# Sparse attention into an MoE layer: 17 pieces of weight conversion in two steps of the first chunk, and w_in's tiles one further ahead of w_out's

## The chip, the cores and the metric

The kernel runs on one core of a Trainium2 chip, with its engines TensorE (PE), VectorE (DVE), ScalarE (ACT), GpSimd (POOL) and SyncE (SP). The metric is the device time of one execution, in microseconds, taken as the median of several runs. Each engine works through its own instructions in order; semaphores tie the engines to each other and to the DMAs.

## What is computed

An attention layer with a block mask feeds a feed-forward layer. 4 batches, 8 heads, 768 positions, head size 64; blocks of 32 positions, each of which sees its neighbours, the first and last block, and three sampled blocks. The inputs are float32 and the weights `w_in` (512 x 2048) and `w_out` (2048 x 512) are too, as the reference stores them:

```python
scores = scale * np.matmul(q, k.transpose(0, 1, 3, 2))
scores = np.where(mask, scores, -1000000000.0)
attn = exp(scores - max) / (sum + 1e-09)
x = np.matmul(attn, v)            # heads joined: 3072 x 512
h = x @ w_in                      # 3072 x 2048
g = h * (1.0 / (1.0 + np.exp(-1.702 * h)))
out = (g @ w_out).astype(np.float32)
```

(The lines of the reference are shortened here.)

## The kernel before

The weights come as 64-bit words, two 32-bit halves each, 128 rows at a time: 16 tiles of w_in and 16 of w_out, 512 KB each (NF = 16). The kernel turns each into float32 and then into a high and a low part for matmuls in fp32r. Every product of the MoE layer is three matmuls: high by high, high by low, low by high.

**Chunks, items, steps.** The 3072 tokens are worked in NC = 6 chunks of 512. The attention of a chunk is a list of items, one for each unit of 64 query rows (the dense edge units have several). The first chunk's items are done ahead (`first`, L658). Then 6 x 16 = 96 MoE steps run, one `tick(m)` each (L618): step m multiplies the chunk by w_in tile m mod 16 (`up`, L482: 12 matmuls, L491 to L493, into PSUM bank 7), applies the gate (`gate`, L496: Tanh on ScalarE at L499, in the first 13 steps a copy of the bank at L504, a product on VectorE at L506), splits the result into ghi (L511, ScalarE) and glo (L519, VectorE), and multiplies the tile of the step before by w_out (`down`, L522: L541, L542, then L537). The attention items of the next chunk are woven between these (`plan`, L579). In the first chunk a new item's scores (L260) come about every second step: steps 1, 3, 5, 7, 9, 11, 12 and 14. Such a step is called heavy here, the others light. An item is four minima on VectorE (L283), four exponentials on ScalarE (L290), eight transposes on TensorE (L306) in the next step, two copies of them (pt, L310), the products with the values (L331), a normalisation (L373), and a turn of the result (L384) whose halves are stored by L391 and L392. The scores go into the two banks that the transposes of the item before went through, so they wait for the copies L310.

**The conversion of the weights.** `weights` (L401 on) is a generator that hands out one small piece of work for each call. Its list `todo` holds the 32 tiles in the order of their conversion: (f, 0) is w_in tile f and (f, 1) is w_out tile f. For the k-th tile it issues, in four calls:

1. the fetch of tile k + 2 (a DMA on ScalarE's queue, L414, into one of three buffers `raw`) and a shift on VectorE (L446, `shift`);
2. the last operation of tile k - 1 (a subtraction on VectorE, L427, `last`), which makes its low part, and, for a w_out tile, the save of its float32 form to DRAM (a DMA on ScalarE's queue, L433, out of the buffer `a`), from where later chunks load it again;
3. a bitwise combination on VectorE (L452, `or`), and on ScalarE the first operation of tile k + 1 (L422), which writes that tile's buffer `a`, one of three in turn;
4. a second combination on VectorE (L456, `or`) and the high part on ScalarE (L459).

The 16 w_in tiles stay in SBUF for good. The w_out tiles go round a ring of WRING = 3. So before it starts w_out tile f the generator asks whether the `down` of tile f - 3 has been issued (L441), and as long as it has not, a call does nothing (L442):

```python
while i == 1 and f - WRING > self.downs - 1:
    yield
```

**How many calls a step makes.** Before the loop, `first` makes 29 calls. In `tick`, n0 calls come ahead of `up`, n1 calls between the gate's ScalarE operations and its VectorE product L506, and n2 calls at the end of the step. A heavy step has no n0. If a tile were not ready in time, `need` (L464) would call the generator until it is. At step 16 what is left is issued at once (L699).

Since the order in which the instructions are issued is the order on each engine, a piece that is issued ahead of another one holds it up on its engine, whether it is urgent or not: the n1 calls stand ahead of the gate's product on VectorE and ahead of ghi on ScalarE, the n2 calls ahead of the next step's work.

Of the kernel before, what the change touches and what calls it, by code (L numbers as in the profile page):

```python
# [27 lines left out]
NF = DF // P  # L28
# [7 lines left out]
WRING = 3  # L36
LAG = 1
# [6 lines left out]
class Kernel:  # L44
# [353 lines left out]
    def weights(self):  # L398

        nc = self.nc  # L400
        todo = []  # L401
        for f in range(NF + LAG):
            if f < NF:
                todo.append((f, 0))
            if f >= LAG:
                todo.append((f - LAG, 1))
        self.ready = set()
        tiles = {}

        def fetch(k):  # L410
            if k < len(todo):
                f, i = todo[k]
                raw = self.work.tile([P, 2 * DM], I32, name="raw", bufs=3)
                nc.scalar.dma_start(out=raw, in_=self.w64[i][f])  # L414
                tiles[k] = {"raw": raw.rearrange("p (a b) -> p a b", b=2)}

        def first(k):


            if k < len(todo):  # L420
                a = tiles[k]["a"] = self.work.tile([P, DM], I32, name="a", bufs=3)
                nc.scalar.activation(out=a.bitcast(F32), in_=tiles[k]["raw"][:, :, 1].bitcast(F32), func=AF.Abs, scale=REBASE)  # L422

        def last(k):
            f, i = todo[k]
            t, w = tiles[k]["t"], tiles[k]["a"].bitcast(F32)
            nc.vector.tensor_tensor(out=t[:, DM:2 * DM], in0=w, in1=t[:, 0:DM].bitcast(F32), op=ALU.subtract)  # L427
            self.ready.add((f, i))

        def save(k):  # L430
            f, i = todo[k]
            if i == 1:
                nc.scalar.dma_start(out=self.ws[f], in_=tiles[k]["a"].bitcast(F32))  # L433
            del tiles[k]

        fetch(0)
        fetch(1)
        yield
        first(0)
        for k, (f, i) in enumerate(todo):  # L440
            while i == 1 and f - WRING > self.downs - 1:  # L441
                yield  # L442
            fetch(k + 2)
            raw, a = tiles[k]["raw"], tiles[k]["a"]
            low, high = raw[:, :, 0], raw[:, :, 1]
            nc.vector.tensor_scalar(out=a, in0=a, scalar1=3, scalar2=None, op0=ALU.logical_shift_left)  # L446
            yield
            if k > 0:
                last(k - 1)
                save(k - 1)  # L450
                yield
            nc.vector.scalar_tensor_tensor(out=a, in0=high, scalar=-0x80000000, in1=a, op0=ALU.bitwise_and,  # L452
                                           op1=ALU.bitwise_or)
            first(k + 1)
            yield
            nc.vector.scalar_tensor_tensor(out=a, in0=low, scalar=29, in1=a, op0=ALU.logical_shift_right,  # L456
                                           op1=ALU.bitwise_or)
            t = tiles[k]["t"] = self.win[f] if i == 0 else self.wout[f % WRING]
            nc.scalar.copy(out=t[:, 0:DM], in_=a.bitcast(F32))  # L459
            yield  # L460
        last(len(todo) - 1)
        save(len(todo) - 1)
# [155 lines left out]
    def tick(self, m):  # L618

        n0, n1, n2 = 0, 0, 0  # L620
        if m < NF:
            heavy = any(part == self.scores for q in range(QT) for part, g in self.at.get(QT * m + q, ()))
            n0, n1, n2 = (0, 3, 3) if heavy else (3, 3, 3)

        def run(n):
            for _ in range(n):
                next(self.conv, None)

        def finish(todo):
            for f in todo:  # L630
                f()

        moe = m < NC * NF
        self.gate_lo(m - 1)
        after = self.begin(QT * m)
        finish(after[:3])
        run(n0)
        finish(after[3:])
        if moe:
            self.up(m, range(0, 2))  # L640
        finish(self.begin(QT * m + 1))
        if moe:
            self.up(m, range(2, 4))
        after = self.begin(QT * m + 2)
        if moe:
            self.gate(m, lambda: run(n1))
        finish(after[:2])
        self.down(m - LAG, 0)
        if moe:
            self.gate_hi(m)  # L650
        finish(after[2:])
        finish(self.begin(QT * m + 3))
        self.down(m - LAG, 1)
        self.split(m + 1)
        self.stream(m + 3)
        run(n2)

    def first(self):  # L658
# [12 lines left out]
        for n, g in enumerate(items):  # L671
            if n == 1:
                next(self.conv)
            exps = self.scores(g)
            exps.pop(0)()
            if n > 1:
                weights(2)
                finish(self.turn(items[n - 2]))
            if n > 0:
                finish(self.transposes(items[n - 1]))  # L680
            finish(exps)
            if n > 0:
                finish(self.values(items[n - 1]))
            self.loads()
            if n > 1:
                weights(2)
# [66 lines left out]
```

## Time and profile before

| | |
|---|---|
| median of 3 runs | 785.84 us (785.08 to 786.23) |
| the profiled execution | 782.75 us |
| its span, first to last instruction | 781.1 us |
| mean granted TensorE clock | 0.984 |

The profile is one execution, with the busy time of each engine, the chain of work that ended last, and each instruction's start. A row of the order of instructions reads: start in us, duration in us, engine, line of the kernel, operation, output <- inputs, shapes, how many were merged, and in brackets the idle time of the engine just before it and what ended it. Durations are from start to the confirmed end, so on one engine the next instruction can start before the end that a row shows. ACTq and SPq are the DMA issues of ScalarE's and SyncE's queues.

### The profile page before, as it was taken

The numbers are of one execution on the slowest core, as the hardware profiler recorded it, in microseconds if no ns is written. First come the engines' busy times: TensorE is split into PE (matmuls) and PEld (weight loads), VectorE is DVE, ScalarE is ACT, GpSimd is POOL, SyncE is SP. The second block draws the span as 40 slices with busy tenths as digits, with TensorE's granted clock in tenths as the row PEclk, the third lists the DMA queues.
The fourth block names the chain that finished last, engine by engine and source line by source line (L and its number), as shares of the span: only waits on it lengthen the run. The fifth ranks groups of instructions, "written<-read, shape, count | busy, mean of one in ns | idle before, by whom it ended". The sixth has DMA issues, their size and how long they took to land.

```text
span 781.1 us, 19264 instructions
## 1 busy us (share of the span) xinstructions
PE 738.6 (95%) x7584; PEld 571.7 (73%) x7584; DVE 412.8 (53%) x1076; ACT 383.5 (49%) x950; POOL 57.1 (7%) x85
## 2 busy tenths in 40 slices
PE   2667999999999999999999999999999999999996
PEld 1445787767777777787877877877777777888884
DVE  3387779887644354445445544444554444443332
ACT  1567667666545444444444544444545454333332
POOL 5122001101000001000000000000000000000000
PEclk9699999999999999999999999999999999999998
DMA  8998887786644437664534465435574321041112
GB/s 267 281 367 296 251 254 256 251 259 222 206 162 153 117 114 219 173 177 129 161 117 145 142 175 156 137 115 163 161 229 153 93 98 42 28 108 40 55 41 55
DMA packets 61117, 128.22 MB, mean 164 GB/s; under 512 B 7569, under 2 KB 26514, under 8 KB 60514
## 3 DMA queue, kind: packets, MB, share of 16 engines
q1 hardware_dynamic: 46882, 80.50, 33.9%
q0 software_dynamic: 7232, 25.51, 10.1%
q10 hardware_dynamic: 6912, 20.97, 8.1%
q8 instruction: 60, 0.98, 0.5%
q14 instruction: 31, 0.25, 0.1%
HBM read 116.47 MB, written 10.49 MB: 163 GB/s over the span
## 4 chain that ended last, share of the span: by engine, by line
PE 78%; DMA 7%; DVE 7%; ACT 4%; issue 2%; SPq 1%; ACTq 0%; DVEq 0%
PE bank L491 11%; PE bank L541 10%; PE bank L542 10%; PE bank L537 10%; PE bank L493 10%; PE bank L492 10%; PE bank L260 5%; PE bank L306 4%; PE bank L331 4%; DMA ws<-a 3%; DMA kg<-in_kb_dram 2%; PE bank L339 2%; PE bank L272 2%; DMA raw<-in_moe_w_in_dram 2%; DVE a L452 1%
## 5 line engine op out<-in xcount | busy, mean ns | idle before, releaser
L491 PE MATMUL bank<-xhi,win 128*128 128x512 f32 x384 | 158.4, 412 | 1.2 <-ACT xhi L391 0.9
L290 ACT ACTIVATE ex<-bank,nm 128x256 f32<-128x256 f32 (+1 forms) x208 | 99.7, 492 | 115.4 <-DVE nm L283 113.6
L506 DVE SCALAR_TENSOR_TENSOR g<-g,bank 128x512 f32<-128x512 f32 x83 | 57.1, 687 | 183.8 <-ACT g L499 183.8
L541 PE MATMUL bank<-wout,ghi 128*128 128x512 f32 x384 | 154.1, 401 | 0.0
L542 PE MATMUL bank<-wout,ghi 128*128 128x512 f32 x384 | 151.7, 395 | 0.0
L493 PE MATMUL bank<-xhi,win 128*128 128x512 f32 x384 | 151.0, 393 | 0.0
L492 PE MATMUL bank<-xlo,win 128*128 128x512 f32 x384 | 150.0, 391 | 0.0
L499 ACT ACTIVATE g<-bank 128x512 f32<-128x512 f32 x96 | 57.5, 599 | 146.4 <-PE bank L493 146.1
L537 PE MATMUL bank<-wout,glo 128*128 128x512 f32 x384 | 107.7, 394 | 0.0
L480 DVE TENSOR_TENSOR wout<-wst,wout 128x512 fp32r<-128x512 f32 x80 | 55.4, 693 | 79.7 <-ACT wout L479 78.7
L511 ACT CAST ghi<-g 128x512 fp32r<-128x512 f32 x96 | 59.7, 622 | 54.6 <-DVE g L506 54.6
L491 PEld LDWEIGHTS bank<-xhi,win 128*128 128x128 f32 x384 | 72.1, 188 | 18.7 <-ACT xhi L391 1.1
L537 PEld LDWEIGHTS bank<-wout,glo 128*128 128x128 f32 x384 | 72.4, 189 | 17.3
L493 PEld LDWEIGHTS bank<-xhi,win 128*128 128x128 f32 x384 | 72.1, 188 | 16.3
L283 DVE CUSTOM_DVE_ANT_1 bank<-bank,bias 128x256 f32<-128x256 f32 x176 | 73.8, 440 | 19.3 <-PE bank L260 16.2
L542 PEld LDWEIGHTS bank<-wout,ghi 128*128 128x128 f32 x384 | 72.5, 189 | 15.6
L541 PEld LDWEIGHTS bank<-wout,ghi 128*128 128x128 f32 x384 | 72.2, 188 | 16.0
L492 PEld LDWEIGHTS bank<-xlo,win 128*128 128x128 f32 x384 | 72.3, 188 | 13.3 <-DVE xlo L392 0.3
L216 POOL DMA_INDIRECT vown<-in_v_dram,vidx x44 | 43.7, 994 | 496.9 <-PE bank L331 385.5
L260 PE MATMUL bank<-kg,qt 64*32 64x256 f32 x1408 | 55.8, 416 | 17.6 <-DMA vmid<-in_v_dram 10.5
L310 ACT COPY pt<-bank 128x512 f32<-128x512 f32 (+1 forms) x120 | 61.1, 563 | 19.4 <-PE bank L306 19.3
L331 PEld LDWEIGHTS bank<-vown,pt 128*32 128x32 f32 x1408 | 43.8, 113 | 31.8 <-ACT pt L310 16.0
(75 smaller groups left out, 821.8 us busy)
## 6 DMA issues: line engine op xcount, KB each, us to landing
wst<-ws SPq DMA_DIRECT2D x80, 256.0 KB, 2.7
kg<-in_kb_dram SPq DMA_DIRECT2D x136, 128.0 KB, 3.2
kg<-in_kb_dram SPq DMA_DIRECT2D x22, 384.0 KB, 4.9
raw<-in_moe_w_in_dram ACTq DMA_DIRECT2D x16, 512.0 KB, 9.7
raw<-in_moe_w_out_dram ACTq DMA_DIRECT2D x16, 512.0 KB, 4.5
kg<-in_kT_dram SPq DMA_DIRECT2D x4, 1536.0 KB
vown<-in_vd_dram SPq DMA_DIRECT2D x8, 768.0 KB, 6.0
qt<-in_q_dram SPq DMA_DIRECT2D x22, 256.0 KB, 4.9
```

What stands on the lines that cost most here:

```text
L260: nc.tensor.matmul(sps[h][BLK * c:BLK * (c + 1), n * i:n * (i + 1)].rearrange("p (n s) -> p n s", s=BLK), self.qt[r][rows, bi, UT * pair + ...
L283: nc.vector.tensor_tensor_reduce(out=at, in0=at, in1=bias, scale=-SCALE, scalar=3.0e38, op0=ALU.add, op1=ALU.min, accum_out=un["nm"][:, ha ...
L290: nc.scalar.activation(out=ex, in_=sps[h][:, n * k:n * (k + 1)], func=AF.Exp, bias=un["nm"][:, half, c:c + 1], scale=-1.0, accum_out=un["r ...
L310: copies.append(lambda pt=pt, ps=ps, m=m: nc.scalar.copy(out=pt[:, 0:m], in_=ps[:, 0:m]))
L331: nc.tensor.matmul(av[BLK * c:BLK * (c + 1), 0, 2 * i + h], g["pt"][h][:, 2 * i + k, BLK * c:BLK * (c + 1)], src[:, at:at + D], start=(k = ...
L491: nc.tensor.matmul(h, wih[:, k], hi[:, k], start=(k == 0), stop=False)
L492: nc.tensor.matmul(h, wih[:, k], lo[:, k], start=False, stop=False)
L493: nc.tensor.matmul(h, wil[:, k], hi[:, k], start=False, stop=(k == NCT - 1))
L511: self.nc.scalar.copy(out=ghi, in_=self.g[m][0])
L537: nc.tensor.matmul(o[n], glo[:, tk[n]], woh, start=False, stop=last)
L541: nc.tensor.matmul(o[n], ghi[:, tk[n]], woh, start=(f == 0), stop=False)
L542: nc.tensor.matmul(o[n], ghi[:, tk[n]], wol, start=False, stop=False)
```

## The change

In the list of tiles, w_out tile f stood behind w_in tile f + 1 (LAG = 1). Now that holds for the first three w_out tiles alone; from the fourth on, w_out tile f stands behind w_in tile f + 2. The list read in0, in1, out0, in2, out1, in3, out2, in4, out3, in5, out4, in6 and so on; now it reads in0, in1, out0, in2, out1, in3, out2, in4, in5, out3, in6, out4, in7 and so on, and ends in15, out13, out14, out15. And the calls at the end of a step, n2, are 4 instead of 3, in heavy and light steps: a heavy and a light step together make 17 calls instead of 15.

```diff
         todo = []
-        for f in range(NF + LAG):
+        lag = lambda f: LAG if f < WRING else LAG + 1
+        for f in range(NF + LAG + 1):
             if f < NF:
                 todo.append((f, 0))
-            if f >= LAG:
-                todo.append((f - LAG, 1))
+            todo += [(k, 1) for k in range(NF) if k + lag(k) == f]
...
-            n0, n1, n2 = (0, 3, 3) if heavy else (3, 3, 3)
+            n0, n1, n2 = (0, 3, 4) if heavy else (3, 3, 4)
```

The ring of three w_out tiles, its check, the three buffers `raw` and the three buffers `a` stay as they are, as do the calls ahead of the loop.

## The prediction

> **What bounds the kernel now.** I read the page first, then the busy time by stretch, then the order of instructions on TensorE, VectorE and ScalarE in the first chunk (MoE steps 0 to 15, about 74 to 203 us), where the change lies.
>
> ```profile
> PE 738.6 (95%) x7584; PEld 571.7 (73%) x7584; DVE 412.8 (53%) x1076; ACT 383.5 (49%) x950; POOL 57.1 (7%) x85
> ```
>
> ```profile
> 92.00:166.00 74.00, 71.91 (x770) 54.96 (x776) 63.80 (x148) 51.48 (x118) 7.01 (x6) 1.00 0.79 253
> ```
>
> The columns are PE, PEld, DVE, ACT, POOL, the granted clock, the DMA share and GB/s. Over the whole span TensorE sets the time (95%) and VectorE is busy for 53%, but in this stretch, while weights are converted, for 63.80 of 74 us (86%). So I looked for the places where TensorE waits in the first chunk. Rows of PE, then of VectorE:
>
> ```profile
> 106.73 1.09 PE L260 MATMUL bank<-kg,qt 64*32 64x256 f32 x32
> 115.45 0.47 PE L491 MATMUL bank<-xhi,win 128*128 128x512 f32 x1
> 121.18 1.09 PE L260 MATMUL bank<-kg,qt 64*32 64x256 f32 x32
> 131.08 0.50 PE L491 MATMUL bank<-xhi,win 128*128 128x512 f32 x1
> 161.12 0.50 PE L491 MATMUL bank<-xhi,win 128*128 128x512 f32 x1
> 165.43 1.58 PE L260 MATMUL bank<-kg,qt 64*32 64x256 f32 x32 [1.30 <-ACT pt L310]
> ```
>
> ```profile
> 94.58 0.43 DVE L283 CUSTOM_DVE_ANT_1 bank<-bank,bias 128x256 f32<-128x256 f32 x1
> 110.94 0.43 DVE L283 CUSTOM_DVE_ANT_1 bank<-bank,bias 128x256 f32<-128x256 f32 x1
> 127.03 0.42 DVE L283 CUSTOM_DVE_ANT_1 bank<-bank,bias 128x256 f32<-128x256 f32 x1
> 141.34 0.42 DVE L283 CUSTOM_DVE_ANT_1 bank<-bank,bias 128x256 f32<-128x256 f32 x1
> 157.07 0.42 DVE L283 CUSTOM_DVE_ANT_1 bank<-bank,bias 128x256 f32<-128x256 f32 x1
> ```
>
> L260 is the scores of a new item (every second step), L491 opens the w_in matmuls of the next step, L283 is the first minimum that VectorE takes of these scores. An undisturbed pair of steps is 121.18 - 106.73 = 14.45 us on TensorE. L283 is queued behind everything that VectorE was given before; I call its distance from L260 the **lag**: 110.94 - 106.73 = 4.21 in step 5, 127.03 - 121.18 = 5.85 in step 7. Behind L283 come the exponentials and then the gate's two reads of the PSUM bank on ScalarE:
>
> ```profile
> 130.43 0.60 ACT L504 COPY wst<-bank 128x512 f32<-128x512 f32 x1
> ```
>
> This copy ends at 131.03, 4.00 us after L283, and the next step's L491, which overwrites that bank, starts at 131.08. Undisturbed, L491 comes 115.45 - 106.73 = 8.72 after the scores. So with a lag above 8.72 - 4.0 = 4.7 TensorE stands still for the difference: 131.08 - 121.18 - 8.72 = 1.18 us in step 7, and about as much before 161.12. The scores at 165.43 then wait 1.30 for the copies of the step before, late in ScalarE's queue. VectorE's five L283 rows are (157.07 - 94.58) / 4 = 15.62 us apart, more than 14.45. **In the first chunk VectorE's queue, with its waits for ScalarE, sets the pace**, and TensorE stalls whenever the lag is used up.
>
> **The change, part by part.** Each call of the generator issues one piece. The pieces on VectorE (rows of 80 to 180 us):
>
> ```profile
> L456 DVE SCALAR_TENSOR_TENSOR a<-raw,a 128x512 int32<-128x512 int32 x22 | 15.1, 687 | 0.5
> L452 DVE SCALAR_TENSOR_TENSOR a<-raw,a 128x512 int32<-128x512 int32 x22 | 15.0, 683 | 0.0
> L446 DVE TENSOR_SCALAR a<-a 128x512 int32<-128x512 int32 x23 | 9.8, 427 | 1.5 <-ACT a L422 1.5
> L427 DVE TENSOR_TENSOR win<-a,win 128x512 fp32r<-128x512 f32 x12 | 8.2, 684 | 2.1 <-ACT win L459 2.1
> ```
>
> A tile is four pieces, 2.48 us by these durations, about 2.25 from start to start; a piece is 0.57 on average. Nothing is removed from the total: 32 tiles stay 32 tiles. I counted the calls through the ring check of L441. Before, the pair of a heavy and a light step has 6 + 9 = 15 calls, all of them used. After, 7 + 10 = 17, of which the ring check empties one in each pair: 16 used, just what two steps consume. Before, nine of the 15 calls of steps 0 and 1 find w_out 3 blocked, and one in step 2 w_out 4. After, w_in 5 stands there, so step 0 does four more pieces and step 1 one more. By step 11 the changed kernel is 9 pieces ahead (4 + 1, and one in each of steps 3, 5, 7, 9), and steps 12 to 14 do that much less. Matmuls wait for no weights in either order: w_out 13, the tightest, is finished in step 13 before, in step 12 after, for use in step 14. The loads move along: w_in 6 is fetched in step 0 instead of step 2.
>
> **Term 1, step 0: a new wait.** ScalarE's L422 of a tile takes the buffer of three tiles earlier (three buffers of a). In the new order the second L422 of step 0 is that of w_out 3, and three tiles before it stands w_out 2, whose buffer is still being saved to DRAM. Before, this ninth tile (then w_in 5) came only in step 1.
>
> ```profile
> 74.42 1.29 ACTq L433 DMA_DIRECT2D ws<-a  x1
> 78.45 0.58 ACT L504 COPY wst<-bank 128x512 f32<-128x512 f32 x1
> 79.78 0.62 ACT L511 CAST ghi<-g 128x512 fp32r<-128x512 f32 x1 [0.76 <-DVE g L506]
> 79.06 0.69 DVE L506 SCALAR_TENSOR_TENSOR g<-g,wst 128x512 f32<-128x512 f32 x1 [1.79 <-ACT wst L504]
> 81.05 0.42 DVE L283 CUSTOM_DVE_ANT_1 bank<-bank,bias 128x256 f32<-128x256 f32 x1
> 82.76 0.40 PE L541 MATMUL bank<-wout,ghi 128*128 128x512 f32 x1
> 85.11 0.69 DVE L506 SCALAR_TENSOR_TENSOR g<-g,wst 128x512 f32<-128x512 f32 x1 [1.86 <-ACT wst L504]
> 86.56 0.48 PE L491 MATMUL bank<-xhi,win 128*128 128x512 f32 x1
> ```
>
> The DMA view of that one issue, and of a later one at 97.83, with the time from issue to landing last:
>
> ```profile
> ws<-a ACTq DMA_DIRECT2D x1, 256.0 KB, 8.4
> ...
> ws<-a ACTq DMA_DIRECT2D x1, 256.0 KB, 5.8
> ```
>
> ```profile
> 70.00:80.00 10.00, 7.95 (x183) 5.76 (x183) 6.46 (x17) 7.34 (x19) 1.96 (x2) 1.00 1.03 345
> ```
>
> The save lands at 74.42 + 8.4 = 82.8, in a stretch whose DMA share is 1.03. L422, issued after the copy of 78.45, holds ScalarE from 79.0 to 82.8; 0.6 later, at 83.4, comes L511 (before: 79.78), for which the w_out matmuls at 82.76 and glo on VectorE wait. L283 came 1.27 after L511, so now at 84.7 instead of 81.05 (+3.65), the copy's end at 88.7, and L491 at 88.7 instead of 86.56: TensorE loses 2.2 us. VectorE's four new pieces of step 0 lie in its idle 1.79 and in the hold, so they cost nothing; without that cover they would cost 2.25. From L506 at 85.11 to L283 at 94.58 were 9.47. One more piece (0.60) lies there, and the wait of this row goes:
>
> ```profile
> 89.50 0.69 DVE L427 TENSOR_TENSOR wout<-a,wout 128x512 fp32r<-128x512 f32 x1 [0.35 <-ACT wout L459]
> ```
>
> So L283 of step 3 comes at 85.11 + 3.65 + 9.47 + 0.60 - 0.35 = 98.5, **3.9 late**. If the save landed before 79.0 instead, only +0.25 would remain; these are the two ends of the term, and I take the row of this very DMA.
>
> The Trainium skill's page "DMA: Bandwidth & Descriptors", section "Anatomy of one DMA", gives a fit of about 2.0 us fixed plus bytes / 436e3 per us. Measured on the GpSimd path, it gives an estimate of 2.6 us for this save: landed at 77.0, no hold. The row's 8.4 disagrees with it, and the measurement decides.
>
> **Term 2, steps 3 to 11.** With 16 pieces to 16 the pieces now fall in the same place in every pair. Heavy: shift, last, or / or, shift, last, or. Light: or, shift, last / or, or / shift, last, or, or. The old trace has each once, heavy in step 9 and light in step 8:
>
> ```profile
> 133.35 0.68 DVE L519 TENSOR_TENSOR glo<-g,ghi 128x512 fp32r<-128x512 f32 x1
> 147.05 0.43 DVE L446 TENSOR_SCALAR a<-a 128x512 int32<-128x512 int32 x1 [0.39 <-ACT a L422]
> 148.08 0.69 DVE L427 TENSOR_TENSOR wout<-a,wout 128x512 fp32r<-128x512 f32 x1 [0.60 <-ACT wout L459]
> 148.69 0.68 DVE L519 TENSOR_TENSOR glo<-g,ghi 128x512 fp32r<-128x512 f32 x1
> ```
>
> Light: 133.35 to 141.34 = 7.99, with the same count. Heavy: 141.34 to 148.69 = 7.35, plus one piece (0.60), less the 0.39 (its buffer is free by then) and 0.25 of the 0.60: 7.3. Together 15.3. To this comes a wait that step 9 lacks. The last piece of a heavy step issues an L422 whose buffer is saved in the same step, about 2.6 us after L283; with 5.8 us to land it starts at 8.4 after L283, where ScalarE would reach it at 6 and VectorE feels it from 7.3 on. Later saves that showed a wait landed between 4.2 and 7.4:
>
> ```profile
> 116.62 0.33 ACTq L433 DMA_DIRECT2D ws<-a  x1
> 138.93 0.36 ACTq L433 DMA_DIRECT2D ws<-a  x1
> 120.84 0.68 ACT L422 ACTIVATE a<-raw 128x512 f32<-128x512 f32 x1 [0.70 <-DMA ws<-a]
> 146.36 0.66 ACT L422 ACTIVATE a<-raw 128x512 f32<-128x512 f32 x1 [1.02 <-DMA ws<-a]
> ```
>
> (4.2 and 7.4 from issue to the released L422.) I charge 0.4 a pair, between nothing and 1.0: a pair is **15.7 us** (15.1 to 16.3, with 0.2 for the two segments' own scatter below), for one piece more than the 15.62 of before. Four pairs: 98.5 + 62.8 = 161.3 for L283 of step 11, 4.2 behind 157.07. TensorE cannot absorb it: step 3's lag is 98.5 less scores at about 94.5 = 4.0, and each pair adds 1.25, so every later pair stalls.
>
> **Term 3, steps 12 to 16.** With nine pieces fewer, TensorE gets something back. The scores wait of 165.43 stays, because ScalarE has the same held L422 ahead of the pt copies (+0.4). The waits of step 14 go, 0.2 ahead of its scores and, as the values L331 start 1.74 after them where an undisturbed L260 row lasts 1.09, 0.65 behind:
>
> ```profile
> 177.87 1.68 PE L260 MATMUL bank<-kg,qt 64*32 64x256 f32 x32 [0.22 <-ACT pt L310]
> 179.61 0.24 PE L331 MATMUL bank<-vown,pt 128*32 128x64 f32 x1
> ```
>
> +0.4 - 0.2 - 0.65 = -0.5. **Sum: +4.2 - 0.5 = +3.7 us.** The profiled execution took 782.75 us (span 781.1 and 1.65 around it); it would become 786.45. The median of the three runs, 785.84, lies 3.1 above it; on that I forecast **789.5 us**.
>
> **The rivals.**
> - *Faster: no hold in step 0.* It decides at one point: whether w_out 2's save lands before 79.0, 4.6 us after its issue, rather than 8.4. Then L283 of step 3 is at 94.8, four pairs of 15.3 bring step 11 to 156.0, 1.1 early, and with -0.5 that is -1.6: 784.2. At most all the stalls shown go: 1.2 in step 7, about 1.1 in step 11, 1.3 and 0.85 in steps 12 and 14, some 4.5 us. For it: later saves landed in 4.2 and 5.8. Against it: the 8.4 is this save's own row, and nothing ahead of it moves. Chance 0.2.
> - *No difference: the hold is there, but the fixed order rids VectorE of its waits.* At 14.9 a pair step 11 is at 98.5 + 59.6 = 158.1, +1.0, and less 0.5 is +0.5: 786.3. For it: the old pair of steps 7 to 9 took 141.34 - 127.03 = 14.31 with 15 pieces. Against it: the save wait above. Chance 0.22.
> - *Slower still: the heavy steps' saves take 7.4 each time.* 16.6 a pair: step 11 at 164.9, +7.8 - 0.5: 793.1. Chance 0.08.
>
> **How the numbers follow.** The forecast has 0.5. With term 2 between 15.1 and 16.3 a pair it reaches from +1.3 to +6.1. The range goes down into the faster rival, -2.3, and up to the +6.1: 783.5 to 791.9. A measurement of this kernel tells 0.2%, 1.6 us, from no change. Faster by more: 0.2, the first rival. Within: 0.22, the second with the forecast's low end standing in for its own edges. Slower: 0.58, the forecast and the third.
>
> **What would show it.** In the changed profile: an L422 in step 0 that waits for ws until about 82.8, with L511 behind it at 83.4; the first w_out matmuls at about 84 and L491 of step 2 near 88.7; L283 of steps 3 to 11 some 15.7 apart, waits of L422 for ws in heavy steps, no matmul that waits for win or wout; idle time on VectorE from step 12 on. The forecast is wrong if L511 of step 0 stays near 80, or if L283 of step 11 comes before 157.

## The result, and the profile after

Over 20 executions each, the changed kernel takes 789.28 us in the median and the kernel before 785.07: a ratio of **1.0059 (95% interval 1.0049 to 1.0069)**, or about 4.6 us slower (the medians themselves lie 4.2 apart). The forecast was 3.7 us slower. The profiled execution of the changed kernel took 789.36 us, with a span of 787.7, 6.6 more than the one before; that execution, of 782.75 us, lies 2.3 below the median of its kernel.

The page's line of busy times, and the view of busy time for the same stretch of the first chunk that the prediction showed:

```profile
PE 741.1 (94%) x7584; PEld 573.1 (73%) x7584; DVE 412.4 (52%) x1076; ACT 383.5 (49%) x950; POOL 57.2 (7%) x85
```

```profile
92.00:166.00 74.00, 71.59 (x750) 53.57 (x749) 65.23 (x151) 51.61 (x118) 7.74 (x6) 1.00 0.82 256
```

VectorE and ScalarE do the same work as before (412.4 and 383.5 us). In this stretch VectorE is busier (65.23 of 74 us, before 63.80) and TensorE starts fewer matmuls (750, before 770). From the scores of step 16 to the end the two profiles take the same time: 787.7 - 195.54 = 592.2 us, before 781.1 - 188.88 = 592.2 (the times of these scores are in the table of the experiments). All of the loss lies ahead of step 16: 1.46 us ahead of the scores of step 1, and 5.2 from there to the scores of step 16.

The order of instructions in step 0, on ScalarE, VectorE and TensorE, and TensorE's first w_in matmul of step 2:

```profile
76.75 0.33 ACTq L433 DMA_DIRECT2D ws<-a  x1
79.92 0.58 ACT L504 COPY wst<-bank 128x512 f32<-128x512 f32 x1
82.00 0.66 ACT L422 ACTIVATE a<-raw 128x512 f32<-128x512 f32 x1 [1.50 <-DMA ws<-a]
82.57 0.60 ACT L511 CAST ghi<-g 128x512 fp32r<-128x512 f32 x1
```

```profile
83.20 0.69 DVE L519 TENSOR_TENSOR glo<-g,ghi 128x512 fp32r<-128x512 f32 x1 [1.38 <-ACT ghi L511]
83.81 0.43 DVE L283 CUSTOM_DVE_ANT_1 bank<-bank,bias 128x256 f32<-128x256 f32 x1
97.91 0.42 DVE L283 CUSTOM_DVE_ANT_1 bank<-bank,bias 128x256 f32<-128x256 f32 x1
114.12 0.42 DVE L283 CUSTOM_DVE_ANT_1 bank<-bank,bias 128x256 f32<-128x256 f32 x1
129.86 0.42 DVE L283 CUSTOM_DVE_ANT_1 bank<-bank,bias 128x256 f32<-128x256 f32 x1
146.16 0.42 DVE L283 CUSTOM_DVE_ANT_1 bank<-bank,bias 128x256 f32<-128x256 f32 x1
162.73 0.42 DVE L283 CUSTOM_DVE_ANT_1 bank<-bank,bias 128x256 f32<-128x256 f32 x1
```

```profile
88.03 0.48 PE L491 MATMUL bank<-xhi,win 128*128 128x512 f32 x1
166.78 0.50 PE L491 MATMUL bank<-xhi,win 128*128 128x512 f32 x1
171.62 0.73 PE L260 MATMUL bank<-kg,qt 64*32 64x256 f32 x2 [1.79 <-ACT pt L310]
```

In this execution the scores of step 1 start 1.46 us later than in the profile before (79.31 against 77.85), so the rows are read from there. (Ahead of the loop TensorE waited 3.39 us for copies pt up to 72.10, in the profile before 1.79 up to 70.50. The tiles converted up to there are the same, so this is not the change.) L422 of w_out 3 waits for the save of w_out 2, as forecast, but the save lands after 5.2 us (76.75 to 82.0) and not after 8.4. L511 comes 3.26 after the scores of step 1 instead of 1.93, the first L283 4.50 instead of 3.20, and TensorE loses nothing in step 2: 88.03 - 79.31 = 8.72, the undisturbed distance. Then the L283 rows of steps 3 to 11 are (162.73 - 97.91) / 4 = **16.20 us** apart, before 15.62. VectorE's rows between them hold 16 pieces a pair, before 15, as the prediction counted (17 are the calls, of which one is emptied). And the scores of step 12 wait 1.79 for the copies pt.

The waits between 78 and 192 us (who waited for whom, sum in us, times, longest), first of the changed kernel, then, from 76 to 186, of the kernel before:

```profile
ACT a L422 <- DMA ws<-a: 9.8, 5, 2.4
DVE wout L427 <- ACT wout L459: 4.0, 4, 1.1
PE bank L260 <- ACT pt L310: 1.8, 1, 1.8
```

```profile
ACT a L422 <- DMA ws<-a: 3.3, 5, 1.0
DVE xlo L392 <- ACT xhi L391: 4.4, 5, 1.2
DVE wout L427 <- ACT wout L459: 3.1, 5, 1.4
```

ScalarE's L422 is held behind saves three times as long as before, and once more, for 2.7 us, behind a fetch. The pair of steps 5 and 6 shows what reaches VectorE of it:

```profile
118.15 0.69 DVE L506 SCALAR_TENSOR_TENSOR g<-g,wst 128x512 f32<-128x512 f32 x1 [0.30 <-ACT wst L504]
120.13 0.69 DVE L427 TENSOR_TENSOR win<-a,win 128x512 fp32r<-128x512 f32 x1 [0.35 <-ACT win L459]
124.12 0.69 DVE L427 TENSOR_TENSOR wout<-a,wout 128x512 fp32r<-128x512 f32 x1 [0.88 <-ACT wout L459]
```

These three are all of VectorE's idle time between 114.12 and 129.86: 1.53 of 15.74 us. The rest, 14.21, is its own work. Taken so over the four pairs, bracketed idle time and the rest, a pair is 13.79 us of work and 1.83 of waits before, and 14.28 and 1.92 after. By this count **the longer pair is nearly all the sixteenth piece** (0.49). The waits did not shrink, they changed their kind: waits for xhi and for the high part of a tile in awkward places went, waits behind a held L422 came.

### The profile page after: what moved, and what is told of

Same layout as the page of the kernel before. It is cut to its first block, busy times and chain, and to the rows that moved or that the text cites. A ratio compares the mean times of both kernels' runs of the same rounds, so it can differ in the third digit from the quotient of the medians.

```text
span 787.7 us, 19282 instructions
## 1 busy us (share of the span) xinstructions
PE 741.1 (94%) x7584; PEld 573.1 (73%) x7584; DVE 412.4 (52%) x1076; ACT 383.5 (49%) x950; POOL 57.2 (7%) x85
## 4 chain that ended last, share of the span: by engine, by line
PE 80%; DMA 8%; DVE 5%; ACT 3%; issue 2%; SPq 1%; ACTq 1%; POOL 0%; POOLq 0%; DVEq 0%
PE bank L491 11%; PE bank L541 10%; PE bank L542 10%; PE bank L537 10%; PE bank L493 10%; PE bank L492 10%; PE bank L306 5%; PE bank L260 5%; PE bank L331 5%; DMA ws<-a 4%; DMA kg<-in_kb_dram 2%; PE bank L339 2%; PE bank L272 2%; DMA raw<-in_moe_w_in_dram 2%; PE bank L384 1%
## 5 line engine op out<-in xcount | busy, mean ns | idle before, releaser
L506 DVE SCALAR_TENSOR_TENSOR g<-g,bank 128x512 f32<-128x512 f32 x83 | 57.0, 687 | 188.0 <-ACT g L499 188.0
L290 ACT ACTIVATE ex<-bank,nm 128x256 f32<-128x256 f32 (+1 forms) x208 | 99.7, 492 | 112.8 <-DVE nm L283 111.8
L283 DVE CUSTOM_DVE_ANT_1 bank<-bank,bias 128x256 f32<-128x256 f32 x176 | 73.8, 440 | 26.3 <-PE bank L260 17.9
L511 ACT CAST ghi<-g 128x512 fp32r<-128x512 f32 x96 | 59.6, 621 | 48.7 <-DVE g L506 48.7
L260 PE MATMUL bank<-kg,qt 64*32 64x256 f32 x1408 | 56.3, 415 | 19.2 <-DMA vmid<-in_v_dram 11.2
L331 PEld LDWEIGHTS bank<-vown,pt 128*32 128x32 f32 x1408 | 44.2, 114 | 33.0 <-ACT pt L310 15.8
```

What stands on the lines that cost most here:

```text
L260: nc.tensor.matmul(sps[h][BLK * c:BLK * (c + 1), n * i:n * (i + 1)].rearrange("p (n s) -> p n s", s=BLK), self.qt[r][rows, bi, UT * pair + ...
L283: nc.vector.tensor_tensor_reduce(out=at, in0=at, in1=bias, scale=-SCALE, scalar=3.0e38, op0=ALU.add, op1=ALU.min, accum_out=un["nm"][:, ha ...
L290: nc.scalar.activation(out=ex, in_=sps[h][:, n * k:n * (k + 1)], func=AF.Exp, bias=un["nm"][:, half, c:c + 1], scale=-1.0, accum_out=un["r ...
L331: nc.tensor.matmul(av[BLK * c:BLK * (c + 1), 0, 2 * i + h], g["pt"][h][:, 2 * i + k, BLK * c:BLK * (c + 1)], src[:, at:at + D], start=(k = ...
L511: self.nc.scalar.copy(out=ghi, in_=self.g[m][0])
```

## The experiments

Twelve kernels. Each is timed beside the kernel before on the same chip and profiled once. The columns after the ratio are from that one profile, in us from its span's start: the scores (L260) of step 1, the first L283 of steps 1, 3 and 11, the scores of step 16; then the mean distance of L283 in steps 3 to 11, and the distance of the scores of step 16 from those of step 1 (the "chunk").

| kernel | ratio to before (95%) | scores 1 | L283 1 | L283 3 | L283 11 | scores 16 | pair | chunk |
|---|---|---|---|---|---|---|---|---|
| before | 1 | 77.85 | 81.05 | 94.58 | 157.07 | 188.88 | 15.62 | 111.0 |
| the change | 1.0059 (1.0049 to 1.0069) | 79.31 | 83.81 | 97.91 | 162.73 | 195.54 | 16.20 | 116.2 |
| order_only | 1.0021 (1.0005 to 1.0038) | 78.41 | 85.42 | 98.92 | 160.46 | 192.26 | 15.39 | 113.8 |
| calls_only | 1.0051 (1.0030 to 1.0072) | 80.32 | 83.52 | 97.58 | 162.98 | 196.46 | 16.35 | 116.1 |
| save_early | 1.0031 (1.0015 to 1.0047) | 82.98 | 86.18 | 100.36 | 163.64 | 194.08 | 15.82 | 111.1 |
| save_fetch_early | 1.0074 (1.0051 to 1.0097) | 78.61 | 84.61 | 98.94 | 165.54 | 196.40 | 16.65 | 117.8 |
| light_extra | 1.0027 (1.0015 to 1.0039) | 79.04 | 86.16 | 100.40 | 164.51 | 193.44 | 16.03 | 114.4 |
| save_loop | 1.0032 (1.0017 to 1.0046) | 84.56 | 87.76 | 102.19 | 167.03 | 198.17 | 16.21 | 113.6 |
| order_save_loop | 1.0017 (1.0005 to 1.0029) | 82.77 | 85.97 | 99.44 | 160.61 | 193.09 | 15.29 | 110.3 |
| before_save_loop | 1.0012 (0.9995 to 1.0029) | 82.83 | 86.03 | 99.50 | 161.53 | 193.69 | 15.51 | 110.9 |
| no_hold0 | 1.0056 (1.0034 to 1.0078) | 80.41 | 83.61 | 97.90 | 162.83 | 193.61 | 16.23 | 113.2 |
| light_no_hold0_save | 1.0017 (0.9997 to 1.0036) | 78.52 | 81.72 | 96.09 | 163.40 | 192.34 | 16.83 | 113.8 |
| light_no_hold0 | 0.9981 (0.9966 to 0.9996) | 79.80 | 83.00 | 97.39 | 160.14 | 189.04 | 15.69 | 109.2 |
| order_no_hold0_save | 0.9997 (0.9978 to 1.0015) | 79.85 | 83.05 | 96.72 | 158.10 | 190.26 | 15.34 | 110.4 |

The ratio is a median over many executions and the other columns are one execution each; a chunk column explains a ratio only to within a microsecond or two. Nor is a pair more exact than some 0.4 us: save_early and save_loop have the same steps 3 to 11, and pairs of 15.82 and 16.21; light_extra and light_no_hold0 too, and 16.03 and 15.69.

Counted as above, the five kernels with 15 pieces in a pair (before, order_only and the three others with 15 calls) have 13.75 to 13.79 us of work and 1.55 to 1.83 of waits in it, the nine with 16 pieces 14.22 to 14.50 and 1.26 to 2.43.

**Theory A**: ScalarE, held by L422 behind the save of the same step, makes the pairs longer. **Theory B**: the sixteenth piece does, by VectorE's own time. **Theory C**: the new order does.

### The two halves of the change apart

order_only keeps the new list and the old calls; calls_only the old list and the new calls.

```diff
 order_only, against the changed kernel
-            n0, n1, n2 = (0, 3, 4) if heavy else (3, 3, 4)
+            n0, n1, n2 = (0, 3, 3) if heavy else (3, 3, 3)
 calls_only, against the kernel before
-            n0, n1, n2 = (0, 3, 3) if heavy else (3, 3, 3)
+            n0, n1, n2 = (0, 3, 4) if heavy else (3, 3, 4)
```

> The new order of the tiles with the old n2 = 3: 15 calls in two steps, all used from step 3 on. Theory A (the cost is ScalarE held by L422 behind the save of the same step, because 16 pieces put the two into one heavy step): the pairs are as far apart as in the kernel before, L283 rows of steps 3 to 11 about 15.6 us, fewer holds; the hold in step 0 stays, some 1 us. Sum 785 to 787 us where before has 785. Theory B (VectorE has one piece more in each heavy step, and the holds only fill idle time): also about 785. Theory C (the new order itself costs): 788 or more.

> The old order of the tiles with the new n2 = 4: by the count of calls, the ring check again empties one call in each pair, and 16 pieces fall in the same places as in the changed kernel, only with other tiles. Theory A and theory B: pairs of about 16.2 us in steps 3 to 11 as after the change, L422 held behind ws by 2 us in heavy steps, no hold in step 0; 787 to 789 us. Theory C: 785.

order_only: 1.0021, about 1.7 us, with pairs of 15.39 us and a hold of 4.0 us in step 0 where 1 was expected; calls_only: 1.0051, about 4.0 us, with pairs of 16.35. So theory C falls for the pairs: **the calls make them longer, the order does not**, and the two halves add up to a little more than the whole. What the order costs fits the hold of step 0, and in order_only's profile it has just the size that the prediction gave it. Its ScalarE rows, and the DMA view of this save (last column: us from issue to landing):

```profile
74.99 1.23 ACTq L433 DMA_DIRECT2D ws<-a  x1
...
79.01 0.58 ACT L504 COPY wst<-bank 128x512 f32<-128x512 f32 x1
83.61 0.66 ACT L422 ACTIVATE a<-raw 128x512 f32<-128x512 f32 x1 [4.02 <-DMA ws<-a]
84.17 0.60 ACT L511 CAST ghi<-g 128x512 fp32r<-128x512 f32 x1
```

```profile
ws<-a ACTq DMA_DIRECT2D x1, 256.0 KB, 8.5
```

The save takes 8.5 us, L422 is held for 4.02, L283 comes 85.42 - 78.41 = 7.0 after its scores, and the scores of step 3 are 2.4 later against those of step 1 than before (16.81 against 14.43). The pairs of 15.39 then give a part of it back.

### The save earlier

save_early issues the save of a w_out tile with its fourth piece; nothing else needs to be done by then. save_fetch_early does the same with the next fetch.

```diff
 save_early, against the changed kernel
                 last(k - 1)
-                save(k - 1)
+                del tiles[k - 1]
...
             nc.scalar.copy(out=t[:, 0:DM], in_=a.bitcast(F32))
+            save(k)
 save_fetch_early, besides
-            fetch(k + 2)
+            if k == 0:
+                fetch(2)
...
+            fetch(k + 3)
```

> The changed kernel, with the save of a w_out tile issued with its fourth piece, two pieces earlier and ahead of the next fetch. Theory A: L422 in heavy steps is no longer held by ws, at most by its own fetch (some 5 us after issue, at about 7.5 us after L283 instead of 8.3); L427 of the light steps waits 0.4 instead of 1.0; pairs 15.3 to 15.8 instead of 16.2, the stall of step 12 smaller by about 1 us; 785 to 787 us. Theory B: the pairs stay at 16 and more, 788 to 790 us.

> As save_early, and the fetch of a tile issued one piece earlier as well, behind the last reader of its buffer. Theory A: no hold of L422 in the heavy steps at all, pairs 15.2 to 15.5 us; 784 to 786 us. Theory B: 788 to 790 us. If save_early is slow and this one is not, the hold was that of the fetch and not that of the save.

save_early: 1.0031. Its chunk is 111.1 us, 5.1 shorter than the changed kernel's and as short as before; L422 waits for its own fetch instead (1.2 to 2.1 us in the four heavy steps), and pairs are 15.82. Theory A has its due: the holds do cost. The median of 787.99 lies at the edge of theory B's time all the same. In the profile the scores of step 1 come at 82.98, 3 to 5 us later than in the kernels that leave the save in its place (L422 waited 2.92 us for its fetch up to 73.09), so a good part is lost ahead of the loop.

save_fetch_early, 1.0074, is a miss for both theories. L422 is held in two of the four heavy steps alone, by 1.2 and 1.1 us, yet the two other pairs take 17.6 and 17.8 us: the DMA issues now stand ahead of the exponentials in ScalarE's queue, and the issue itself waits. In light_no_hold0_save (below) the same happened once; its ScalarE rows:

```profile
115.82 0.33 ACTq L433 DMA_DIRECT2D ws<-a  x1
116.26 0.47 ACT L290 ACTIVATE ex<-bank,nm 128x256 f32<-128x256 f32 x1 [3.49 <-DMA kg<-in_kb_dram]
```

The exponentials wait 3.49 us for an issue that needed no data after 112.8. What that issue waited for (the profile names a load of another queue that ended then) stays open.

### The sixteenth piece, with the hold moved

light_extra leaves heavy steps at 6 calls and gives light ones 10. No call is emptied from step 3 on, so a pair has 16 pieces as in the changed kernel; but the L422 behind the save comes after the copies pt.

```diff
-            n0, n1, n2 = (0, 3, 4) if heavy else (3, 3, 4)
+            n0, n1, n2 = (0, 3, 3) if heavy else (3, 3, 4)
```

> The changed kernel with calls of (0, 3, 3) in heavy and (3, 3, 4) in light steps: 16 calls and 16 pieces in a pair, none emptied by the ring check from step 3 on, so VectorE has the same pieces in a pair as after the change. The L422 that takes the buffer of the save in the same heavy step comes one call later, in the light step behind the copies pt. Theory A (that L422 holds pt and the high part of w_out): pairs 15.3 to 15.8 us instead of 16.2, 786 to 788 us. Theory B (16 pieces are too many for VectorE): pairs 16.0 and more, 788 to 790 us.

The pairs stay at 16.03, theory B's number; the median of 787.15 is theory A's. (light_no_hold0 below, with the same steps 3 to 11, has pairs of 15.69, which is theory A's, so this run does not decide between the two.) The holds are still there (13.5 us in all, against 9.8), but they reach VectorE as 0.9 us in two of four pairs, through L446. What gets better is the end: from L283 of step 11 to the scores of step 16 it is 193.44 - 164.51 = 28.9 us, against 195.54 - 162.73 = 32.8 in the changed kernel and 31.8 before. The copies pt of step 12 are no longer behind a held L422, and the scores of step 12 do not wait for them. (Some 1.5 us of the 32.8 are the granted clock: see term 3 below.) The ratio is 1.0027, 0.32% less than the change's, in spite of a hold of 4.1 us in step 0 of the profile.

### The early save in the loop only

Three kernels take the early save from w_out 2 on: the changed kernel (save_loop), order_only (order_save_loop) and the kernel before (before_save_loop).

```diff
                 last(k - 1)
-                save(k - 1)
+                if k - 1 < 6:
+                    save(k - 1)
...
             nc.scalar.copy(out=t[:, 0:DM], in_=a.bitcast(F32))
+            if k >= 6:
+                save(k)
```

> As save_early (the changed kernel, the save issued with the tile's fourth piece), but only from w_out 2 on, so that what is issued ahead of the loop stays as it was but for that one save. Theory A: pairs as in save_early, 15.8 us, with L422 of heavy steps held by their own fetch by 1 to 2 us; step 0 held less than 1.5 us; the loss that save_early had ahead of the loop is gone: 785 to 787 us. Theory B: 788 us and more.

> The new order with the old n2 = 3, and the save with the fourth piece from w_out 2 on. If order_only's 1.7 us over before are the hold of step 0, that hold shrinks from 4.0 us to 2 or less, first L283 at 3.2 to 5 us after the scores instead of 7.0, pairs about 15.3 us; 784 to 786 us. If they are not, 787 us.

> The kernel before, and only the save with the fourth piece from w_out 2 on. Its holds behind ws (0.35 to 1.0 us) go; by theory A pairs 15.2 to 15.5 instead of 15.6 and 783.5 to 785.5 us; by theory B no difference, 785 to 786 us.

All three miss the times that theory A gave them: 1.0032 (788.18 us, theory B's), 1.0017, 1.0012. The chunks of the two with 15 calls are as short as expected or nearly (110.3 and 110.9); but in all three the scores of step 1 come at 82.8 to 84.6, against 77.9 to 80.4 in the kernels that leave w_out 2's save alone. That the moved save did this is not shown. Rows of ScalarE ahead of the loop, of save_loop and then of before_save_loop:

```profile
63.31 0.45 ACTq L433 DMA_DIRECT2D ws<-a  x1
74.65 0.66 ACT L422 ACTIVATE a<-raw 128x512 f32<-128x512 f32 x1 [6.05 <-DMA ws<-a]
79.26 0.33 ACTq L433 DMA_DIRECT2D ws<-a  x1
```

```profile
75.88 0.33 ACTq L433 DMA_DIRECT2D ws<-a  x1
76.25 1.40 ACTq L414 DMA_DIRECT2D raw<-in_moe_w_in_dram  x1
77.70 0.37 ACT L391 CAST xhi<-bank 128x256 fp32r<-128x256 f32 x1 [1.96 <-issue]
```

In save_loop ScalarE stands for 6.05 us, and in order_save_loop for 3.30, behind the save of w_out 1, which neither kernel moves; w_out 2's save is issued only afterwards (79.26 and 77.56). In before_save_loop the fetch issued right behind the moved save holds ScalarE for 1.96 us. And save_fetch_early, which moves the same save, has its scores of step 1 at 78.61. save_loop's profile is the slowest of its twelve executions besides (792.02 us). What the three lost against their expectations stays open.

save_loop shows what a pair is when the hold is too short to reach VectorE (L422 at 142.22 waits 1.13 us for its fetch). VectorE's idle rows of this pair, from 135.11 to 150.33 = 15.22 us (in this kernel's file L446 is L445, and the gate's L504 and L506 are L505 and L507):

```profile
139.14 0.69 DVE L507 SCALAR_TENSOR_TENSOR g<-g,wst 128x512 f32<-128x512 f32 x1 [0.30 <-ACT wst L505]
141.12 0.69 DVE L427 TENSOR_TENSOR win<-a,win 128x512 fp32r<-128x512 f32 x1 [0.35 <-ACT win L459]
144.58 0.69 DVE L427 TENSOR_TENSOR wout<-a,wout 128x512 fp32r<-128x512 f32 x1 [0.35 <-ACT wout L459]
```

1.00 us idle and 14.22 of work. The pair just before it, with L422 held for 2.1 us by its fetch, has 1.05 instead of the last 0.35, and the pair that begins at 102.19, held for 3.0, has 0.87 at L446 besides, and takes 16.87.

### Step 0 without its hold

In the last four the step-0 calls are (3, 2, 0), so that w_out 3's L422 is issued in step 1, behind the exponentials. no_hold0 is the changed kernel with that alone; light_no_hold0 is light_extra with it; the other two also save early, from w_out 3 on (k >= 7), and leave w_out 2's save where it was.

```diff
+            if m == 0:
+                n0, n1, n2 = 3, 2, 0
```

> The changed kernel with calls (3, 2, 0) in step 0 alone, so that the L422 of w_out 3 is issued in step 1 behind the exponentials, when the save of w_out 2 has landed. If the hold of step 0 is a cost of its own: first L283 3.2 us after its scores instead of 4.5, L511 of step 0 1.9 us after them instead of 3.3; steps 1 to 16 some 1.5 us shorter than in the changed kernel (116.2), pairs 16.2 as there; 787 to 788 us. If VectorE's later pace swallows it: no difference, 789 us.

> As light_no_hold0_save, but the saves where they were. L446 of the light steps then waits some 0.9 us in two of the four pairs, as in light_extra: pairs 15.6 to 16.0, about 110 us from step 1 to step 16; 783 to 786 us.

> light_extra with step 0 as in no_hold0, and the saves from w_out 3 on with the fourth piece. No hold left ahead of pt, ghi or the exponentials. Pairs 15.2 to 15.5 us (VectorE's own 14.4 and some 1.0 of short waits), steps 11 to 16 in 29 us as in light_extra; from the scores of step 1 to those of step 16 about 108 us, where the kernel before has 111.0 and the changed one 116.2; 781 to 784 us. By theory B (the sixteenth piece in a pair cannot be paid for) 786 us and more.

> order_only (15 calls) with step 0 as in no_hold0 and the saves from w_out 3 on with the fourth piece; what is issued ahead of the loop stays as in order_only. Pairs 15.3 us, steps 11 to 16 in 32 us as with all 15-call kernels: 110 us from step 1 to step 16; 784 to 785.5 us. If order_save_loop's 786.8 came from its save ahead of the loop, this one is 1 to 2 us faster than it; if not, the same.

no_hold0: the hold is gone (L283 3.20 after its scores, L511 1.94) and the chunk is 3.0 us shorter in its profile (1.1 of it up to L283 of step 3, 2.0 from L283 of step 11 on), but the median is not: 1.0056. Its executions lie between 786.5 and 795.2 us, too wide for 1.5 us to be told. The price of the hold in the changed kernel by itself stays open.

light_no_hold0: **0.9981 (0.9966 to 0.9996), the only one faster than the kernel before**, by 0.2%, and 0.8% faster than the change. It meets its expectation in time and pairs, and has the change's order and 16 pieces in a pair. Its L283 rows of steps 3 and 11, and the scores of step 12:

```profile
97.39 0.43 DVE L283 CUSTOM_DVE_ANT_1 bank<-bank,bias 128x256 f32<-128x256 f32 x1
160.14 0.43 DVE L283 CUSTOM_DVE_ANT_1 bank<-bank,bias 128x256 f32<-128x256 f32 x1
```

```profile
167.14 1.11 PE L260 MATMUL bank<-kg,qt 64*32 64x256 f32 x32
```

15.69 a pair, and no wait of the scores of step 12. The pairs are still longer than TensorE's 14.45; the gain lies in steps 11 to 16 (28.9 us instead of 31.8), where 17 pieces are left behind L283 of step 11, as in the changed kernel, and 26 in the kernel before.

order_no_hold0_save, 0.9997, meets its expectation, and lies 0.2% below order_save_loop; but the two intervals overlap, so that w_out 2's early save costs these 0.2% is not shown. light_no_hold0_save, 1.0017, misses: two more L422 waits of 1.5 and 2.3 us for fetches, and the pair of 18.53 us with the late issue above.

## Why the prediction was right, step by step

**What bounds the kernel: right.** From the scores of step 16 on, the time is the same 592.2 us to within 0.1 us; ahead of it VectorE's queue sets the pace. With lags of 114.12 - 108.20 = 5.9 in step 5 up to 162.73 - 156.00 = 6.7 in step 11 in the changed kernel (scores of its steps 5, 7, 9 and 11 at 108.20, 123.92, 139.68 and 156.00), TensorE stood still in every pair from step 5 on: the scores are 15.72, 15.76 and 16.32 us apart, and not 14.45.

**Term 1, the hold of step 0: the mechanism right, the size wrong in the execution profiled.** The prediction took 8.4 us for the save, 3.65 us for L283 of step 1 and 3.9 for that of step 3. Measured: 5.2 us for the save, and against the scores of step 1, 1.3 and 1.9 us (97.91 - 79.31 = 18.60, before 16.73). In order_only and light_extra the hold was 4.0 and 4.1 us, as forecast. The save's time is no constant: in the profile before and in order_only it was issued 0.55 us behind a fetch of 512 KB, in the changed kernel's 1.85 us, and there the DMA engines were less full (no run separates these two differences):

```profile
70.00:80.00 10.00, 7.29 (x112) 5.92 (x118) 7.06 (x19) 7.58 (x20) 1.97 (x2) 0.83 0.82 279
```

0.82 against 1.03 (column before the last; in order_only 1.04). One DMA's row is the price in one execution. The range went down to the case without a hold, and so covers both.

The Trainium skill's page "DMA: Bandwidth & Descriptors", section "Queues, rings and completion order", says that each DMA engine takes turns between the queues at the grain of packets and works a ring in order. A save behind a fetch on the same ring, in a stretch that other queues fill, should be late by that; the 8.4 and 8.5 us agree, but no run shows the turns or the ring themselves. The same page's fit, made on the GpSimd path (an estimate of 2.6 us), is met by none of the three.

**Term 2, a pair of 15.7: right in kind, too small.** The 15.3 that the prediction put together from step 8 and step 9 of the old trace are 15.22 in the pairs of save_early and save_loop where the hold did not reach VectorE. The hold was charged at 0.4 and costs about 1.0: 16.20 - 15.22. The saves land as late as thought, but L422 then starts 7.8 to 8.7 us after L283 in all four pairs (once behind its fetch), and the copies pt and the high part of w_out come after it in ScalarE's queue. By step 11 the errors of terms 1 and 2 cancel, which is luck: 4.2 us behind in the forecast, and 83.42 - 79.22 = 4.2 measured, counted from the scores of step 1.

**Term 3, steps 12 to 16: the step that failed.** The forecast gave 0.5 us back; measured it is a loss of 1.0 (32.81 against 31.81). The waits of step 14 did go (0.75 us less from the scores of step 14 to those of step 16). The same held L422 ahead of pt, charged at 0.4, put off the scores of step 12 by 0.53 (171.62 - 162.73 = 8.89 behind L283 of step 11, before 8.36), much as charged:

```profile
165.32 0.46 ACTq L433 DMA_DIRECT2D ws<-a  x1
170.44 0.66 ACT L422 ACTIVATE a<-raw 128x512 f32<-128x512 f32 x1 [1.73 <-DMA ws<-a]
171.00 1.06 ACT L310 COPY pt<-bank 128x512 f32<-128x512 f32 x2
```

The other 1.2 us lie between the scores of step 12 and those of step 14 (13.66, before 12.44). Nothing waits for pt there, since its second copy ends at 172.06 and the products start at 174.00, right behind the scores. But TensorE ran slowly. The busy time behind the scores of step 12, of the changed kernel, the kernel before and save_early (granted clock in the third column from the end):

```profile
172.00:175.00 3.00, 3.00 (x72) 1.67 (x74) 2.49 (x6) 1.93 (x5) 0.00 (x0) 0.50 0.02 5
166.00:169.00 3.00, 3.00 (x100) 2.20 (x99) 2.79 (x5) 2.18 (x5) 0.00 (x0) 1.00 0.90 284
172.00:175.00 3.00, 3.00 (x99) 2.10 (x98) 2.53 (x8) 2.00 (x5) 0.00 (x0) 1.00 0.33 29
```

The granted clock was 0.50 in the changed kernel, and a product L331 of this step took 0.31 us where it took 0.24 before. save_early, save_fetch_early, save_loop and no_hold0 have the same pieces in these steps and a clock of 1.00, and take 12.11 to 12.16 us for them: the clock cost some 1.5 us, and without it term 3 would have come out as forecast. So the step that failed is that a stall was priced by its length alone. The clock fell behind the wait of 1.79 us, and in calls_only behind one of 2.51; in the kernel before it did not fall behind 1.30, in save_loop not behind 1.64. A limit can't be read from that: ahead of the loop, light_extra's TensorE waited 2.14 us up to 72.23 and the clock stayed at 1.00. How often it fell in the twenty executions, one profile does not tell. light_extra and light_no_hold0, where this L422 comes after pt, do these steps in 28.9 us, without the wait and with a clock of 1.00.

**The sum.** The forecast of 789.5 us lies 0.2 from the median of 789.28. That is closer than its terms deserve: terms 1 and 2 are off in opposite directions, term 3 has the wrong sign, and the three runs it stands on had a median 0.8 above that of the twenty.

**The rivals.** The rival that ends faster put its whole weight on w_out 2's save. Without the hold at all the kernel is still slower (no_hold0, 1.0056), since the pairs stay at 16.2: the rival's condition would not have been enough. The rival of no difference needed pairs of 14.9; no 16-piece kernel averages less than 15.69. The slower one needed saves of 7.4 us and pairs of 16.6: in the three pairs of steps 3 to 11 where the save held L422, it had landed 4.7 to 5.8 us after its issue.

## What to carry to other kernels

When an engine off the critical path has used up its lead, one more piece of work in each period costs its own time (0.49 us here), even where the total stays the same, unless the waits shrink by as much (light_no_hold0, 1.26 us of waits a pair instead of 1.83): look for the stretch in which it is the bound, and not at its share of the span. Where a buffer comes round, find the DMA that empties it and count the pieces between that issue and the next writer; here an in-order ScalarE turned a 5 to 8 us save into a stall for everything behind the writer, and moving the writer behind the urgent copies (light_extra, 1.0027) was worth about as much as an earlier save (save_early, 1.0031); with the writer of step 0 moved too, the kernel became faster than before (light_no_hold0, 0.9981). Moving a DMA issue forward can put a wait in front of work that had none. And where TensorE stalls longer than before, read the granted clock right behind the stall: here 0.5 us more of a stall came with some 1.5 us lost at half the clock.

## What the hardware showed that was not expected

A save of 256 KB took 5.2 us in one execution and 8.4 and 8.5 in two others, with the same instructions ahead of it but for the weights that the fetch brings. The granted clock of TensorE read 0.50 for 3 us behind a stall of 1.79 us (172 to 175 in the changed kernel), and 1.00 behind one of 2.14 in light_extra. And a DMA issue on ScalarE's queue held the exponentials behind it for 3.5 us (light_no_hold0_save), though its data had long been ready.
